# Sliding attention beside a gated MLP on one core: statistics, loads and transposes of the first tiles rearranged, and the output matmuls in another order

## The chip, the core and the metric

The kernel runs on one core of a Trainium2 chip. The core has five instruction streams that run side by side and wait for each other through semaphores: TensorE (PE: matmuls, and the loads of their weights, PEld), VectorE (DVE), ScalarE (ACT), GpSimd (POOL) and SyncE (SP, which here only issues DMAs). Matrices lie in SBUF with 128 partitions; matmuls write into PSUM, eight banks of 512 float32 columns per partition. The metric is the device time of one execution in microseconds (us), as the median of several. The profile's span is a little shorter than that time, since it starts with the first recorded work of the program.

## What is computed

`x` has 2048 tokens of 512 channels, in bfloat16, and is normalised once (`xn`). Two branches read it, and both are added to `x`.

```python
def _A_ref(x, wqkv, wo):                     # H = 32 heads of 16 channels
    W, dil = (8, 2)                          # each token sees itself and 7 tokens back, in steps of 2
    qkv = (x @ wqkv) ...
    logits = jnp.einsum('bhsd,bhswd->bhsw', q, kg) * scale
    attn = _softmax(logits, axis=-1)
    o = jnp.einsum('bhsw,bhswd->bhsd', attn, vg)
    return o ... @ wo

def _B_ref(x, w_in, w_sp, b_sp, w_out):      # F = 1376, Fh = 688
    z = _gelu(jnp.einsum('bsd,df->bsf', x, w_in))
    z1 = z[..., :Fh].copy()
    z2 = _layernorm(z[..., Fh:], axis=-1)
    g = jnp.einsum('ts,bsf->btf', w_sp, z2) + b_sp[None, :, None]
    return jnp.einsum('bsf,fd->bsd', z1 * g, w_out)
x = A_x
xn = _layernorm(x, axis=-1)
return x + _A_ref(xn, A_wqkv, A_wo) + _B_ref(xn, B_w_in, B_w_sp, B_b_sp, B_w_out)
```

## The kernel before

The tokens are 16 tiles of 128. Nothing is scheduled by a planner: each engine runs its instructions in the order in which the program text issues them (`manual_schedule`), and the tile framework adds the semaphore waits. Instructions of different engines are interleaved in the text so that a wait is short. [...]

**The front (lines 90 to 182 and 350 to 383).** SP loads tile 0, tile 1, tiles 2 and 3 together (`x0`), then `w_z2` (the right half of `w_in`, 688 KB), then tiles 4 to 7, the two halves of `wqk`, and the other tiles. ScalarE's own queue loads `b16`, which is `b_sp` as 16 rows of 128. While nothing has arrived, TensorE runs matmuls of a tile of ones (`spin`). For each of the first four tiles: `ln_stats(i)` takes mean and variance on DVE (`bn_stats`, `bn_aggr`), `roots` takes the square root on ScalarE, `recip` and `ln_apply` (DVE) make the normalised tile, `transpose_pe` turns it with four matmuls into PSUM, and a copy (ScalarE for tiles 0 and 1, DVE for 2 and 3) writes `xnT`, channels by tokens. As soon as `xnT` of a tile exists, TensorE runs its eight matmuls with `w_z2` (`z2_part`, four channel chunks times two halves of 344 columns); `z2_gelu` on ScalarE stores Gelu of the sum. PSUM for these comes from `bank_pair`, three pairs of banks in turn. `b16` is turned by a TensorE transpose (`pb`) and copied to `b_col`, one value of `b_sp` per partition for each tile.

Tiles 4 to 15 go in pairs (`groups`): statistics on DVE, an inverse root by Newton steps on DVE and POOL (`ln_newton`), and a transposing DMA on SP.

**The middle (lines 401 to 531 and 590 to 611).** Q and K (`qk_pair`, `qk_chunk`), the remaining `z2` tiles, V, the attention products, and then for each of the 16 output tiles `mix(j)` (32 matmuls with `w_sp`, which SP loads transposed as `wspT`; ScalarE adds `b_col`) and `z1_tile(j)` (eight matmuls and Gelu). `gate_out` multiplies the two on DVE and sends the product by a transposing DMA to `uT`. `vector_work` spreads the weighted sum over V on DVE between these (`av_ops`); its result is `op`, with channels grouped by position in the head. `op_rest` copies two of the 16 positions into free rows of the sixth chunk of `uT`, by eight DMAs: for the first half of the tokens on SP (line 610), for the second on ScalarE's queue (line 657).

**The output stage (lines 614 to 659).** Each output tile of 128 tokens is one PSUM bank. It gets two parts. The attention part (line 635) is 14 matmuls of 32 rows; four tiles use the four row groups of the array at once (`tile_position`), each tile in its own bank. The other part (line 646) is six full matmuls of `uT` with `wout`. Tiles are numbered by `jj` (0 to 3) and row group `k` (0 to 3). Before, a pair of `jj` is worked on at a time: attention parts of both (112 matmuls), then the full matmuls of its eight tiles, each followed by an add of `x` on DVE (line 650) and a store. So the two kinds of matmul alternate: 112 row-packed, 48 full, 112 row-packed, 42 full, and the last tile apart (`last_tile`, in two halves of 256 columns). `xr` holds the rows of `x` to add, two buffers; `ot` the results, four buffers; `rest` adds the attention part and `x` of the last tile ahead of time.

Of the kernel before, what the change touches and what calls it, by code (L numbers as in the profile page):

```python
# [7 lines left out]
BF16 = mybir.dt.bfloat16  # L8
# [37 lines left out]
def kernel(  # L46
# [42 lines left out]

    b16 = const.tile([NT, P], BF16, name="b16")  # L90
    A.dma_start(b16[:], B_b_sp.rearrange("(j p) -> j p", p=P))


# [4 lines left out]
    def spin(n):  # L98
        for _ in range(n):
            PE.matmul(idle[:, 0, 0:P], ones[:], ones[:], start=True, stop=True)  # L100

    spin(26)

# [6 lines left out]
    for c in range(C):  # L110
# [7 lines left out]
                    base=-DIL * (W - 1), pattern=[[DIL, W], [1, HALO]], channel_multiplier=0)  # L118
    b_col = const.tile([P, NT], F32, name="b_col")
    stats = const.tile([P, NT, 6], F32, name="stats")  # L120
    mv = const.tile([P, NT, 2], F32, name="mv")
# [48 lines left out]
    SP.dma_start(x0[:, 1, :], x2[P:2 * P, :])  # L170
    SP.dma_start(x0[:, 2:4, :], x2[2 * P:4 * P, :].rearrange("(i p) d -> p i d", p=P))
    SP.dma_start(w_z2[:], w_in_r[:, :, FH:F])
    xq.append(x0)
    load_x(1)
# [174 lines left out]

    pb = ps_aux.tile([P, NT], BF16, name="pb", tag="aux")  # L350
    PE.transpose(pb[:], b16[:], ident[0:NT, 0:NT])
    spin(9)
    ln_stats(0)
    roots(0, 1)
    A.copy(b_col[:], pb[:])
    ln_stats(1)
    roots(1, 2)
    recip(0)
    transpose_pe(0, ln_apply(0))
    recip(1)  # L360
    spin(4)
    transpose_pe(1, ln_apply(1))
    spin(4)
    ln_stats(2)
    roots(2, 3)
    ln_stats(3)
    roots(3, 4)
    pz0 = z2_start(0)
    z2_gelu(0, pz0)
    recip(2)  # L370
    xn2 = ln_apply(2)
    recip(3)
    xn3 = ln_apply(3)
    pz1 = bank_pair("pzb")
    for kc in range(2):
        z2_part(1, pz1, kc)
    transpose_pe(2, xn2)
    for kc in range(2, C):
        z2_part(1, pz1, kc)
    transpose_pe(3, xn3)  # L380
# [7 lines left out]
    for g in groups + (None,):  # L388
        if g:
            for i in range(*g):  # L390
                ln_stats(i)
            ln_newton(*g)
        if prev:
            for i in range(*prev):
                transpose_dma(i, ln_apply(i))
            if prev[0] == 6:
                SP.dma_start(wv[:], wqkv_r[:, :, 2 * D:3 * D])
        prev = g
# [17 lines left out]
    z2_square(5)  # L416
    qk_chunk(1, 3)
    for j in range(5):
        load_wsp(j)
        if j == 1:  # L420
            SP.dma_start(w_z1[:], w_in_r[:, :, 0:FH])
# [192 lines left out]
    def last_tile(i, rest):  # L614

        ot = otp.tile([P, D], BF16, name="ot")
        for h in range(2):
            ns = slice(h * D // 2, (h + 1) * D // 2)
            po = ps_o[0].tile([P, D], F32, name="po")
# [3 lines left out]
            V.tensor_tensor(ot[:, ns], po[:, ns], rest[:, ns], ALU.add)  # L623
            SP.dma_start(out2[i * P:(i + 1) * P, ns], ot[:, ns])


    ps_o.append(ctx.enter_context(tc.tile_pool(name="ps_o1", bufs=4, space=PSUM, side="right", reuse_waits="tile")))
    for pair in range(2):
        pos = {}
        for jj in (2 * pair, 2 * pair + 1):  # L630
            for k in range(NG):
                pos[jj, k] = ps_o[jj % 2].tile([P, D], F32, name="po")
            for d in range(DHA):
                for k in range(NG):
                    PE.matmul(pos[jj, k][:], op[32 * k:32 * k + 32, d, jj * P:(jj + 1) * P],  # L635
                              wo_r[32 * k:32 * k + 32, d, :],
                              start=(d == 0), stop=((jj, k, d) == (3, NG - 1, DHA - 1)), tile_position=(32 * k, 0))
        for jj in (2 * pair, 2 * pair + 1):
            hb, q = jj // 2, jj % 2
            for k in range(NG):  # L640
                i = 8 * hb + 2 * k + q
                if (jj, k) == (3, NG - 1):
                    last_tile(i, rest)
                    continue
                for m in range(MCH):
                    PE.matmul(pos[jj, k][:], uT[:, m, i * P:(i + 1) * P], wout[:, m, :],  # L646
                              start=False, stop=(m == MCH - 1))
                vector_work(2.0)
                ot = otp.tile([P, D], BF16, name="ot")
                V.tensor_tensor(ot[:], pos[jj, k][:], xrs[jj][:, k, :], ALU.add)  # L650
                SP.dma_start(out2[i * P:(i + 1) * P, :], ot[:])
                if (jj, k) == (2, 0):
                    rest = pwp.tile([P, D], F32, name="rest", tag="pw")
                    V.tensor_tensor(rest[:], pos[3, NG - 1][:], xrs[3][:, NG - 1, :], ALU.add)
            if jj == 0:
                vector_work(1e9)
                op_rest(1, A)
            if jj + 2 < 4:
                load_xr(jj + 2)


# [28 lines left out]
```

## Time and profile before

| | |
|---|---|
| time, median of 3 runs | 206.86 us (206.8 to 207.03) |
| time of the profiled execution | 206.6 us |
| its span | 204.9 us |
| TensorE busy | 200.3 us, 98% |
| VectorE busy | 166.1 us, 81% |
| ScalarE busy | 93.5 us, 46% |
| first matmul that the result needs (`pt`, transposes of tile 0) | 5.33 us |
| first z2 matmul (`pzb`) | 6.83 us |
| first q/k matmul (`pq`) | 11.94 us |
| output stage begins (`po`, row-packed) | 168.64 us |

The profile gives, for one execution, the instructions of each engine with start and duration from the span's start. Matmuls are pipelined: a recorded matmul of 512 columns lasts 0.38 us, but the next one starts 0.216 later, so on TensorE the distance from start to start counts. The chain of waits follows the work that ended last back to the start: what stands in it sets the end. What an engine off that chain does costs nothing until it makes the chain wait. The timeline merges equal neighbours ("x4" is four instructions), and in brackets says how long the engine was idle before and what it waited for.

### The profile page before, as it was taken

The numbers are of one execution on the slowest core, as the hardware profiler recorded it, in microseconds if no ns is written. First come the engines' busy times: TensorE is split into PE (matmuls) and PEld (weight loads), VectorE is DVE, ScalarE is ACT, GpSimd is POOL, SyncE is SP. The second block draws the span as 40 slices with busy tenths as digits, with TensorE's granted clock in tenths as the row PEclk, the third lists the DMA queues.
The fourth block names the chain that finished last, engine by engine and source line by source line (L and its number), as shares of the span: only waits on it lengthen the run. The fifth ranks groups of instructions, "written<-read, shape, count | busy, mean of one in ns | idle before, by whom it ended". The sixth has DMA issues, their size and how long they took to land.

```text
span 204.9 us, 4056 instructions
## 1 busy us (share of the span) xinstructions
PE 200.3 (98%) x1660; PEld 120.7 (59%) x1666; DVE 166.1 (81%) x192; ACT 93.5 (46%) x145; POOL 16.1 (8%) x82
## 2 busy tenths in 40 slices
PE   7999999999999999999999999999999999999994
PEld 7755554555566666656666666666666664444442
DVE  4899949659299599989999999999999985582353
ACT  3868897676879996335733331213333320000000
POOL 5045630000000000100000000000000000000000
PEclk9999999999999999999999999999999999999999
DMA  6973846999000004718766799999565225047323
GB/s 170 363 223 78 198 95 154 213 212 117 4 3 0 3 0 44 154 32 163 122 129 141 179 210 187 218 175 187 114 145 140 56 48 80 26 99 218 110 99 97
DMA packets 67395, 25.64 MB, mean 125 GB/s; under 512 B 57152, under 2 KB 67248, under 8 KB 67248
## 3 DMA queue, kind: packets, MB, share of 16 engines
q1 hardware_dynamic: 66960, 25.24, 57.6%
q8 instruction: 13, 0.21, 0.4%
q10 hardware_dynamic: 416, 0.14, 0.3%
q14 instruction: 6, 0.05, 0.1%
HBM read 9.79 MB, written 2.10 MB: 58 GB/s over the span
## 4 chain that ended last, share of the span: by engine, by line
PE 96%; DVE 1%; DMA 1%; issue 0%
PE pg L492 36%; PE pq L260 10%; PE po L646 9%; PE pzb L229 9%; PE pz L504 9%; PE pv L285 7%; PE po L635 6%; PE pl L310 4%; PE pq L272 3%; DMA xq<-in_A_x_dram 1%; PE po L621 1%; PE pt L212 1%; DVE stats L185 1%; PE idle L100 0%; DVE xn L190 0%
## 5 line engine op out<-in xcount | busy, mean ns | idle before, releaser
L492 PE MATMUL pg<-z,wspT 128*128 128x344 bf16 x512 | 77.3, 309 | 0.0
L492 PEld LDWEIGHTS <-wspT 128*128 128x128 bf16 x512 | 50.0, 98 | 24.9 <-issue 0.4
L301 DVE TENSOR_TENSOR pr<-qk 128x8192 bf16<-128x8192 bf16 x8 | 35.0, 4420 | 7.4 <-PE pl L310 7.4
L495 ACT ACTIVATE gs<-pg,b_col 128x688 bf16<-128x688 f32 x16 | 13.3, 833 | 52.9 <-PE pg L492 52.9
L558 DVE TENSOR_TENSOR pw<-vp,a_sb 128x4096 bf16<-128x4096 bf16 x16 | 36.1, 2284 | 0.0
L650 DVE TENSOR_TENSOR ot<-po,xr 128x512 bf16<-128x512 f32 x15 | 10.2, 689 | 15.2 <-PE po L646 14.9
L260 PE MATMUL pq<-xnT,wqk 128*128 128x512 bf16 x93 | 21.4, 379 | 0.2
L504 PE MATMUL pz<-w_z,xnT 128*128 128x344 bf16 x128 | 21.3, 309 | 0.0
L229 PE MATMUL pzb<-w_z,xnT 128*128 128x344 bf16 x128 | 20.1, 309 | 0.0
L646 PE MATMUL po<-wout,uT 128*128 128x512 bf16 x88 | 19.3, 379 | 0.3 <-issue 0.3
L563 DVE TENSOR_TENSOR pw<-pw 128x4096 bf16<-128x4096 bf16 x8 | 18.3, 2288 | 0.1
L229 PEld LDWEIGHTS <-xnT 128*128 128x128 bf16 x128 | 12.3, 98 | 7.0 <-issue 0.4
L504 PEld LDWEIGHTS <-xnT 128*128 128x128 bf16 x128 | 12.4, 98 | 6.5 <-issue 0.4
L260 PEld LDWEIGHTS <-wqk 128*128 128x128 bf16 x96 | 9.3, 98 | 10.9 <-issue 0.4
L646 PEld LDWEIGHTS <-uT 128*128 128x128 bf16 x90 | 8.6, 98 | 11.0 <-issue 0.8
L263 ACT CAST qk<-pq 128x1024 bf16<-128x1024 f32 x12 | 12.1, 1012 | 5.4 <-PE pq L260 5.4
L285 PE MATMUL pv<-xnT,wv 128*32 128x512 bf16 x256 | 14.6, 380 | 0.0
L509 ACT ACTIVATE z<-pz 128x688 bf16<-128x688 f32 x16 | 11.9, 743 | 5.6 <-PE pz L504 5.2
L238 ACT ACTIVATE junk<-z 128x688 bf16<-128x688 bf16 x16 | 12.4, 778 | 0.2
L635 PE MATMUL po<-wo_r,op 32*128 32x512 bf16 x224 | 12.4, 375 | 0.0
L234 ACT ACTIVATE z<-pzb 128x688 bf16<-128x688 f32 x16 | 11.8, 735 | 1.4 <-PE pzb L229 1.4
L285 PEld LDWEIGHTS <-wv 128*32 128x32 bf16 x256 | 9.4, 139 | 4.6 <-issue 0.3
(81 smaller groups left out, 169.2 us busy)
## 6 DMA issues: line engine op xcount, KB each, us to landing
xr<-in_A_x_dram SPq DMA_DIRECT2D x4, 512.0 KB, 4.1
out_dram<-ot SPq DMA_DIRECT2D x15, 128.0 KB, 1.8
wo_r<-in_A_wo_dram SPq DMA_DIRECT2D x4, 448.0 KB, 4.8
w_z<-in_B_w_in_dram SPq DMA_DIRECT2D x2, 688.0 KB, 4.9
xq<-in_A_x_dram SPq DMA_DIRECT2D x2, 512.0 KB, 7.0
wqk<-in_A_wqkv_dram SPq DMA_DIRECT2D x2, 512.0 KB, 7.0
wout<-in_B_w_out_dram SPq DMA_DIRECT2D x1, 640.0 KB, 5.2
a_sb<-in_A_x_dram SPq DMA_DIRECT2D x1, 512.0 KB, 9.1
```

Source lines behind the costliest of these rows:

```text
L229: PE.matmul(pz[:, hh, 0:FHALF], xnT[:, kc, i * P:(i + 1) * P], w_z2[:, kc, hh * FHALF:(hh + 1) * FHALF], start=(kc == 0), stop=(kc == C - 1))
L238: A.activation(junk[:], z2[:, i, :], ACT.Square, accum_out=zsq[:, i:i + 1])
L260: PE.matmul(pq[:, s, :], wqk[:, kc, s, c * P:(c + 1) * P], xnT[:, kc, tsl], start=(kc == 0), stop=(kc == C - 1))
L285: PE.matmul(pv[32 * k:32 * k + 32, dd, :].rearrange("p (b t) -> p b t", b=NB), wv_v[:, kc, 2 * d2 + dd, :], xnT_g[:, kc, :, k, :], start=( ...
L301: V.tensor_tensor(pr[:], qk[hb][:, 0, :, HALO:HALO + SB].unsqueeze(1).broadcast_to([P, 2, C, SB]), shifted(qk[hb][:, 1, :, off:off + SB]), ...
L492: PE.matmul(pg[:, hh, 0:FHALF], wsps[j][:, k, :], z2[:, k, hh * FHALF:(hh + 1) * FHALF], start=(k == 0), stop=(k == NT - 1))
L495: A.activation(gs[:], pg[:, :, 0:FHALF], ACT.Identity, bias=b_col[:, j:j + 1])
L504: PE.matmul(pz[:, hh, 0:FHALF], xnT[:, kc, j * P:(j + 1) * P], w_z1[:, kc, hh * FHALF:(hh + 1) * FHALF], start=(kc == 0), stop=(kc == C - 1))
L558: V.tensor_tensor(pw[:], shifted(vp[:, :, hb, off:off + P]), a_sb[:, 2 * p:2 * p + 2, osl].unsqueeze(2).broadcast_to([P, 2, DH, P]), ALU.mult)
L563: V.tensor_tensor(pws[p - 1][:], pws[p - 1][:], pw[:], ALU.add)
L635: PE.matmul(pos[jj, k][:], op[32 * k:32 * k + 32, d, jj * P:(jj + 1) * P], wo_r[32 * k:32 * k + 32, d, :], start=(d == 0), stop=((jj, k, d ...
L646: PE.matmul(pos[jj, k][:], uT[:, m, i * P:(i + 1) * P], wout[:, m, :], start=False, stop=(m == MCH - 1))
```

## The change

The diff has three parts.

Front: tile 3 is loaded by itself, after `w_z2`. The mean and variance of tile 1 are taken on ScalarE with two activations that add up along the row (Identity with scale −1/512 gives the negative mean; Square with that as bias gives the summed squared deviations), and its normalisation adds the negative mean. A square root of a constant is ScalarE's first instruction. The order of the first tiles' instructions is new: on TensorE, the first four z2 matmuls of tile 0 stand before the transposes of tile 1, and two more before those of tile 2. `ln_stats(4)` is moved ahead. The idle matmuls are 35 and 5, where there were 26, 9, 4 and 4.

`b_sp`: no DMA on ScalarE's queue and no transpose on TensorE; a transposing DMA on SP, placed after the twelve transposing DMAs of `xnT` and before the loads of `wspT`, and a copy on POOL.

Output stage: the full matmuls of the eight tiles of `jj` 0 and 1 come first, then the attention parts of all four `jj` in one row of 224 matmuls, then the full matmuls of the other tiles. The adds and stores of `jj` 0 and 1 follow their attention part. All of DVE's remaining attention work and the second `op_rest` stand before the first add. The last tile is as it was.

```diff
@@ -87,9 +87,6 @@
         pool = ps_b if turn[0] % 3 == 0 and not two else ps_a
         return pool.tile([P, 2, 512], F32, name=name, tag="mm")
 
-    b16 = const.tile([NT, P], BF16, name="b16")
-    A.dma_start(b16[:], B_b_sp.rearrange("(j p) -> j p", p=P))
-
 
     ones = const.tile([P, P], BF16, name="ones")
     V.memset(ones[:], 1.0)
@@ -99,7 +96,7 @@
         for _ in range(n):
             PE.matmul(idle[:, 0, 0:P], ones[:], ones[:], start=True, stop=True)
 
-    spin(26)
+    spin(35)
 
     ident = const.tile([P, P], BF16, name="ident")
     G.memset(ident[:], 0.0)
@@ -117,6 +114,7 @@
     G.affine_select(out=mask[:], in_=mask[:], compare_op=ALU.is_ge, fill=NEG,
                     base=-DIL * (W - 1), pattern=[[DIL, W], [1, HALO]], channel_multiplier=0)
     b_col = const.tile([P, NT], F32, name="b_col")
+    b_t = const.tile([P, NT], BF16, name="b_t")
     stats = const.tile([P, NT, 6], F32, name="stats")
     mv = const.tile([P, NT, 2], F32, name="mv")
     rstd = const.tile([P, NT], F32, name="rstd")
@@ -168,8 +166,9 @@
     x0 = xqp.tile([P, 4, D], BF16, name="xq")
     SP.dma_start(x0[:, 0, :], x2[0:P, :])
     SP.dma_start(x0[:, 1, :], x2[P:2 * P, :])
-    SP.dma_start(x0[:, 2:4, :], x2[2 * P:4 * P, :].rearrange("(i p) d -> p i d", p=P))
+    SP.dma_start(x0[:, 2, :], x2[2 * P:3 * P, :])
     SP.dma_start(w_z2[:], w_in_r[:, :, FH:F])
+    SP.dma_start(x0[:, 3, :], x2[3 * P:4 * P, :])
     xq.append(x0)
     load_x(1)
     for s in range(2):
@@ -347,36 +346,37 @@
     def recip(i):
         V.reciprocal(rstd[:, i:i + 1], rstd[:, i:i + 1])
 
-    pb = ps_aux.tile([P, NT], BF16, name="pb", tag="aux")
-    PE.transpose(pb[:], b16[:], ident[0:NT, 0:NT])
-    spin(9)
+    A.activation(zrstd[:, 0:1], eps_t[:], ACT.Sqrt)
     ln_stats(0)
+
+    A.activation(junk[:, 0:D], x0[:, 1, :], ACT.Identity, scale=-1.0 / D, accum_out=mv[:, 1, 0:1])
     roots(0, 1)
-    A.copy(b_col[:], pb[:])
-    ln_stats(1)
-    roots(1, 2)
+    A.activation(junk[:, 0:D], x0[:, 1, :], ACT.Square, bias=mv[:, 1, 0:1], accum_out=mv[:, 1, 1:2])
+    A.activation(rstd[:, 1:2], mv[:, 1, 1:2], ACT.Sqrt, bias=eps_t[:], scale=1.0 / D)
     recip(0)
     transpose_pe(0, ln_apply(0))
+    spin(5)
+    ln_stats(2)
     recip(1)
-    spin(4)
-    transpose_pe(1, ln_apply(1))
-    spin(4)
-    ln_stats(2)
+    xn1 = xnp.tile([P, D], BF16, name="xn")
+    V.tensor_scalar(xn1[:], x0[:, 1, :], mv[:, 1, 0:1], rstd[:, 1:2], ALU.add, ALU.mult)
     roots(2, 3)
+    pz0 = bank_pair("pzb")
+    for kc in range(2):
+        z2_part(0, pz0, kc)
+    transpose_pe(1, xn1)
+    recip(2)
+    xn2 = ln_apply(2)
     ln_stats(3)
     roots(3, 4)
-    pz0 = z2_start(0)
+    z2_part(0, pz0, 2)
+    transpose_pe(2, xn2)
+    z2_part(0, pz0, 3)
     z2_gelu(0, pz0)
-    recip(2)
-    xn2 = ln_apply(2)
     recip(3)
     xn3 = ln_apply(3)
-    pz1 = bank_pair("pzb")
-    for kc in range(2):
-        z2_part(1, pz1, kc)
-    transpose_pe(2, xn2)
-    for kc in range(2, C):
-        z2_part(1, pz1, kc)
+    ln_stats(4)
+    pz1 = z2_start(1)
     transpose_pe(3, xn3)
     z2_gelu(1, pz1)
     z2_tile(2)
@@ -388,7 +388,8 @@
     for g in groups + (None,):
         if g:
             for i in range(*g):
-                ln_stats(i)
+                if i > 4:
+                    ln_stats(i)
             ln_newton(*g)
         if prev:
             for i in range(*prev):
@@ -415,6 +416,8 @@
     qk_chunk(1, 2)
     z2_square(5)
     qk_chunk(1, 3)
+    SP.dma_start_transpose(b_t[:], B_b_sp.rearrange("(j p) -> j p", p=P))
+    G.tensor_copy(b_col[:], b_t[:])
     for j in range(5):
         load_wsp(j)
         if j == 1:
@@ -614,51 +617,67 @@
     def last_tile(i, rest):
 
         ot = otp.tile([P, D], BF16, name="ot")
-        for h in range(2):
-            ns = slice(h * D // 2, (h + 1) * D // 2)
+        for q, n0, n1 in ((SP, 0, 256), (SP, 256, 512)):
+            ns = slice(n0, n1)
             po = ps_o[0].tile([P, D], F32, name="po")
             for m in range(MCH):
                 PE.matmul(po[:, ns], uT[:, m, i * P:(i + 1) * P], wout[:, m, ns],
                           start=(m == 0), stop=(m == MCH - 1))
             V.tensor_tensor(ot[:, ns], po[:, ns], rest[:, ns], ALU.add)
-            SP.dma_start(out2[i * P:(i + 1) * P, ns], ot[:, ns])
+            q.dma_start(out2[i * P:(i + 1) * P, ns], ot[:, ns])
+
 
 
     ps_o.append(ctx.enter_context(tc.tile_pool(name="ps_o1", bufs=4, space=PSUM, side="right", reuse_waits="tile")))
-    for pair in range(2):
-        pos = {}
-        for jj in (2 * pair, 2 * pair + 1):
+    pos = {}
+
+    def tokens_of(jj, k):
+        return 8 * (jj // 2) + 2 * k + jj % 2
+
+    def out_b(jj, k, first):
+        i = tokens_of(jj, k)
+        if first:
+            pos[jj, k] = ps_o[jj % 2].tile([P, D], F32, name="po")
+        for m in range(MCH):
+            PE.matmul(pos[jj, k][:], uT[:, m, i * P:(i + 1) * P], wout[:, m, :],
+                      start=first and m == 0, stop=not first and m == MCH - 1)
+
+    def out_a(jj, first):
+        for k in range(NG):
+            if first:
+                pos[jj, k] = ps_o[jj % 2].tile([P, D], F32, name="po")
+        for d in range(DHA):
             for k in range(NG):
-                pos[jj, k] = ps_o[jj % 2].tile([P, D], F32, name="po")
-            for d in range(DHA):
-                for k in range(NG):
-                    PE.matmul(pos[jj, k][:], op[32 * k:32 * k + 32, d, jj * P:(jj + 1) * P],
-                              wo_r[32 * k:32 * k + 32, d, :],
-                              start=(d == 0), stop=((jj, k, d) == (3, NG - 1, DHA - 1)), tile_position=(32 * k, 0))
-        for jj in (2 * pair, 2 * pair + 1):
-            hb, q = jj // 2, jj % 2
+                PE.matmul(pos[jj, k][:], op[32 * k:32 * k + 32, d, jj * P:(jj + 1) * P],
+                          wo_r[32 * k:32 * k + 32, d, :], start=first and d == 0,
+                          stop=(not first or (jj, k) == (3, NG - 1)) and d == DHA - 1, tile_position=(32 * k, 0))
+
+    def store(jj, k):
+        i = tokens_of(jj, k)
+        ot = otp.tile([P, D], BF16, name="ot")
+        V.tensor_tensor(ot[:], pos[jj, k][:], xrs[jj][:, k, :], ALU.add)
+        SP.dma_start(out2[i * P:(i + 1) * P, :], ot[:])
+
+    for jj in range(2):
+        for k in range(NG):
+            out_b(jj, k, True)
+    vector_work(1e9)
+    op_rest(1, A)
+    for jj in range(4):
+        out_a(jj, jj > 1)
+        if jj < 2:
             for k in range(NG):
-                i = 8 * hb + 2 * k + q
-                if (jj, k) == (3, NG - 1):
-                    last_tile(i, rest)
-                    continue
-                for m in range(MCH):
-                    PE.matmul(pos[jj, k][:], uT[:, m, i * P:(i + 1) * P], wout[:, m, :],
-                              start=False, stop=(m == MCH - 1))
-                vector_work(2.0)
-                ot = otp.tile([P, D], BF16, name="ot")
-                V.tensor_tensor(ot[:], pos[jj, k][:], xrs[jj][:, k, :], ALU.add)
-                SP.dma_start(out2[i * P:(i + 1) * P, :], ot[:])
-                if (jj, k) == (2, 0):
-                    rest = pwp.tile([P, D], F32, name="rest", tag="pw")
-                    V.tensor_tensor(rest[:], pos[3, NG - 1][:], xrs[3][:, NG - 1, :], ALU.add)
-            if jj == 0:
-                vector_work(1e9)
-                op_rest(1, A)
-            if jj + 2 < 4:
-                load_xr(jj + 2)
-
-
+                store(jj, k)
+            load_xr(jj + 2)
+    rest = pwp.tile([P, D], F32, name="rest", tag="pw")
+    V.tensor_tensor(rest[:], pos[3, NG - 1][:], xrs[3][:, NG - 1, :], ALU.add)
+    for jj in range(2, 4):
+        for k in range(NG):
+            if (jj, k) == (3, NG - 1):
+                last_tile(tokens_of(jj, k), rest)
+            else:
+                out_b(jj, k, False)
+                store(jj, k)
```

## The prediction

> **What bounds the kernel now.** I read the page's shares and chain first, then the chain in order of time, then the timeline of the two places that the change touches. Page and chain:
>
> ```profile
> PE 200.3 (98%) x1660; PEld 120.7 (59%) x1666; DVE 166.1 (81%) x192; ACT 93.5 (46%) x145; POOL 16.1 (8%) x82
> PE 96%; DVE 1%; DMA 1%; issue 0%
> ```
>
> ```profile
> 4.86 0.42 DVE xn L190
> ...
> 5.33 0.61 PE pt L212 x4
> 5.94 0.43 PE idle L100 x4
> 6.37 0.26 PE pt L212 x4
> 6.63 0.22 PE idle L100 x4
> 6.85 1.90 PE pzb L229 x12
> ...
> 168.71 6.16 PE po L635 x112
> 174.87 0.16 issue
> 175.03 10.31 PE po L646 x47
> 185.33 6.15 PE po L635 x112
> 191.49 0.16 issue
> 191.65 9.01 PE po L646 x41
> ```
>
> From 6.85 to 201.98 the chain never leaves TensorE. Time can be won only by (a) starting the useful stream before 6.85, (b) taking matmuls or gaps out of it. It can be lost by any new wait in it. Now the front by timeline:
>
> ```profile
> 1.26 0.42 SPq L170 DMA_DIRECT2D xq<-in_A_x_dram  x1
> ...
> 2.19 0.47 SPq L172 DMA_DIRECT2D w_z<-in_B_w_in_dram  x1
> ...
> 4.02 0.29 ACT L194 ACTIVATE rstd<-mv,eps_t 128x1 f32<-128x1 f32 x1 [1.49 <-DVE mv L186]
> ...
> 4.69 0.13 DVE L348 RECIPROCAL rstd<-rstd 128x1 f32<-128x1 f32 x1
> ...
> 6.63 1.76 PEld L229 LDWEIGHTS <-xnT 128*128 128x128 bf16 x12
> 6.83 1.91 PE L229 MATMUL pzb<-w_z,xnT 128*128 128x344 bf16 x12
> ```
>
> Two things meet at 6.8. The weights from xnT are loaded at 6.63, when ScalarE's copy is done, but the matmul starts at 6.83. The DMA list gives w_z2 4.6 us from issue to landing: 2.19 + 4.6 = 6.79. So w_z2 ends last, 0.2 behind xnT of tile 0. Also, rstd of tile 0 is there at 4.31, but its reciprocal waits until 4.69 behind tile 1's statistics on DVE.
>
> **The change, part by part.**
>
> *Tile 1's statistics to ScalarE.* DVE loses bn_stats and bn_aggr of tile 1 (0.66 + 0.18). ScalarE gains a spare root at the start (0.29, behind the table load, before any data), an Identity and a Square with accumulators, and no longer copies b_col (0.17). Tile 1 lands at 1.26 + 2.2 = 3.46. No row shows Identity over 512 elements with an accumulator. Nearest: Square over 688 (0.78, its accumulator read starting 0.68 in and taking 0.19) and the copy of 512 (0.585). I take 0.63 and 0.10 for the part of the read that follows. Tile 0's root then starts at 4.19 instead of 4.02 and ends at 4.48. Its reciprocal no longer queues behind anything on DVE: 4.50 instead of 4.69. All that follows moves by 0.19: normalised tile 4.67, transposes 5.14, copy on ScalarE 5.79, xnT of tile 0 at 6.42 (was 6.61). Bounds: with the 688 rows unscaled (0.87 together) the root is 0.14 later and the gain 0.05; with 0.585 and no read after it, 0.33. Square and the second root end near 5.5, ahead of that copy.
>
> [...]
>
> *w_z2 ahead of tile 3.* Tiles 2 and 3 landed at 1.72 + 3.2 = 4.92, the 688 KB of w_z2 1.87 later, so 128 KB less ahead is worth 0.35 us: landing at about 6.45. It could be less, as the transfer is issued no earlier (2.19) and the queue ran at only 98 GB/s from 3.1 to 3.6, waiting for issues: between 0.15 and 0.35, I take 0.31. Tile 3 lands at about 6.8 instead of 4.92. Only its bn_stats waits for it, in DVE's order behind tile 2's normalisation, which ends near 7.3: hidden by 0.5. SP issues one DMA more (0.42), so tiles 4 to 7, wqk and the two later groups are issued 0.42 later. The first wqk half landed about 3.25 + 7.0 = 10.25; with 0.42 it is 10.7, and TensorE wants it at 11.9.
>
> *First z2 matmul.* Both inputs now arrive at 6.42 to 6.48: it starts at about 6.50, 0.33 earlier.
>
> *From there to the q/k matmuls (11.94 now).* The stretch before held 32 matmuls at 0.146 and eight transposes at 0.055: 4.67 + 0.44 = 5.11, exactly 6.83 to 11.94, no waits. The new order holds twelve transposes there, since tile 1's moved from the covered time into the stream: 5.33, so 11.83. Waits: transposes of tile 1 at 7.08 (its input is ready near 6.44) end at 7.47; ScalarE's copy (0.63) gives xnT at 8.13. z2 of tile 1 would start at 8.11, so it starts at about 8.20: 0.09 lost. Tile 2's normalised input (7.3) is wanted at 7.6, tile 3's (9.1) at 9.4. The Gelu table load moves from 7.76 to about 8.5, the first Gelu ends near 10.55, and its bank is wanted at 10.75. Sum: 11.92 against 11.94. The front gives **0.02**: the 0.33 is spent on 0.22 of transposes that had been free and 0.09 of a new wait. Bounds: 0.25 gained (landing and statistics at their better ends, copy in 0.42 as DVE does it) to 0.2 lost.
>
> *b_sp.* The ACT-queue DMA, TensorE's transpose and the copy go; SP issues one more transposing DMA before the first wspT, POOL one small copy. On SP such a DMA takes 5.36 / 4 = 1.34. Behind it stand five wspT loads (from 31.85) and w_z1, the first wanted at 73.3: nothing, and 1.3 without that cover. POOL's next instruction, a memset for the gate, is 40 us away.
>
> *The output stage.* Matmul counts stay: 224 row-packed, 88 full. Start to start, 168.64 to 185.27 holds 28 rounds of four and eight tiles: 16.63. From 185.27 to the last tile at 200.50 it holds 28 rounds and seven tiles: 15.23. One tile is 1.296 (residual adds at 194.22, 195.52, 196.81), so the first has 0.10 more: the step back into packed mode. 15.23 − 7 × 1.296 = 6.16 for 28 rounds; at the full matmul's pitch of 0.216 they are 6.05, so stepping out costs 0.11. One pair of steps goes: **0.21**. Bounds: 0, if packed rounds are really slower and the step in was a bank waiting for DVE; 0.52, if all of the 0.42 idle of the weight loader before L646 is a step.
>
> New waits there: full matmuls of tiles 0 to 7 now start at 168.6 and need op rows that SP issues from 159.76 to 164.78 and lands 1.8 later: 2 us of cover at the start. DVE's last products (2.28 + 2.28 + 1.22 from 170.01) end at 175.8; the packed stretch starts at 179.0. Its third part takes over the first part's banks 6.05 after the stretch began; four residual adds start 3.2 in and take 2.5, end 5.7: 0.3 of cover. The second four need ot buffers whose stores were issued 2.3 earlier and land in 1.8: 0.5 of cover. The x rows of the last four tiles are issued near 188.2 and land at 192.3; the early sum for the last tile waits for them on DVE about a microsecond, and DVE has caught up two tiles later at 1.3 per tile against 0.69. The tail is unchanged.
>
> **Sum.** 0.02 + 0.21 = 0.23 off. The profiled execution took 206.6 (span 204.9, 1.7 around it), 0.26 under the median of 206.86; I carry the saving over: **206.6**. Its own range is 206.1 to 207.05 (0.77 gained to 0.2 lost). A difference under 0.2% (0.41 us) is about what a measurement of this kernel can't tell from no change.
>
> **Rivals.**
> *The front passes through.* The earlier start reaches the q/k matmuls (0.25) and two mode steps are worth 0.3: 0.55, 206.3. For it: w_z2 was the last arrival, and all terms are at bounds that rows allow. Against: four transposes are no longer covered. 0.25.
>
> *No part does what it says.* If rounds are slower in themselves and the front's gain is spent: 206.85. 0.1.
>
> *TensorE warms up later: slower.* Weight loads of the idle matmuls take 0.15 until 6.2 and 0.10 after:
>
> ```profile
> 6.05 0.15 PEld L212 LDWEIGHTS <-xn 128*128 128x128 bf16 x1
> ...
> 6.41 0.10 PEld L100 LDWEIGHTS <-ones 128*128 128x128 bf16 x1
> ```
>
> The array runs at half pace for some 5.1 us from its first matmul (1.12). Before, matmuls filled the time up to 6.83. Now five idle ones end near 6.1 and nothing follows until 6.5, just where the pace changed. If the change comes x later, x / 2 is lost; over 0.41 from x = 1.3. Starting anew it would be 5.1 later: 209.1. Against it: gaps of 0.3 near 5.0 were there before as well. 0.08.
>
> [...]
>
> *Stores too slow: slower.* If the stores land in 3.1 (as the op rows on ACT's queue do) instead of 1.8, the second four adds are 0.8 late and the fourth packed part waits: 207.4. 0.06.
>
> The forecast itself has 0.51, mostly within 0.2%. Faster: 0.25 plus a small part of the forecast's lower edge, 0.28; slower: 0.14; within: 0.58. The range 206.1 to 207.1 leaves out the two slower cases and little else.
>
> **What would show it.** First z2 matmul near 6.5; first q/k matmul at 11.8 to 12.0 (under 11.7 the front passes through, over 12.3 the clock or a wait); ScalarE's first Identity near 3.5 and tile 0's root near 4.2; one packed stretch of 12.2 with no gap at its third and fourth part; its start at 179.0. I am wrong if TensorE idles inside that stretch, or if the first loads after 6.5 still take 0.15.

## The result, and the profile after

The changed kernel takes 207.63 us (median of 21 executions, 206.99 to 209.42) against 206.78 (21 executions, 206.47 to 207.96) on the same chip: a ratio of 1.0044, 95% interval 1.0028 to 1.0059. It is 0.85 us slower, outside the range of the prediction. Its profiled execution took 207.34, span 205.6 (before: 206.6 and 204.9).

The page's shares and the tail of the chain of waits in order of time (start, length, what):

```profile
PE 200.7 (98%) x1662; PEld 120.9 (59%) x1662; DVE 165.5 (80%) x190; ACT 94.8 (46%) x149; POOL 17.7 (9%) x83
...
PE 93%; DMA 4%; DVE 1%; SPq 1%; issue 0%; DVEq 0%
```

```profile
179.25 5.67 PE po L651 x101
184.93 2.77 DMA out_dram<-ot
187.72 0.05 DVEq L658
187.77 1.29 DVE ot L658 x2
189.11 3.18 PE po L651 x53
```

TensorE is still busy 98% of the span, so the shares show nothing. The chain does: it leaves TensorE in the middle of the packed stretch. A store of the output lands, two residual adds follow, and only then do the last 53 packed matmuls start. The timeline of the same place:

```profile
179.18 9.70 PE L651 MATMUL po<-wo_r,op 32*128 32x512 bf16 x171
...
182.41 2.48 DVE L658 TENSOR_TENSOR ot<-po,xr 128x512 bf16<-128x512 f32 x4 [6.35 <-PE po L651]
183.13 3.11 SPq L659 DMA_DIRECT2D out_dram<-ot  x4
185.43 0.69 DVE L658 TENSOR_TENSOR ot<-po,xr 128x512 bf16<-128x512 f32 x1 [0.54 <-PE po L651]
...
187.17 1.89 DVE L658 TENSOR_TENSOR ot<-po,xr 128x512 bf16<-128x512 f32 x3 [1.04 <-DMA out_dram<-ot]
...
189.11 3.18 PE L651 MATMUL po<-wo_r,op 32*128 32x512 bf16 x53 [0.23 <-DVE ot L658]
```

The first four adds run in one piece. Of the second four one runs, and the next waits 1.04 for its `ot` buffer: there are four, and it is the sixth add, so it needs the second store to have landed. The chain names the fourth store (launched at 184.93), because the wait for it ended just before the add at 187.77. But from 187.17 on the adds start 0.60 apart, as the first four do, so it is the second store's landing that sets them. The fourth packed part takes the banks that these adds free. From the start of the stretch (179.18) to the next full matmul (192.22) it is 13.04; without the hole it is 12.20 in an experiment below, so the hole is 0.84.

The front in the same view:

```profile
2.18 0.43 SPq L170 DMA_DIRECT2D w_z<-in_B_w_in_dram  x1
...
3.45 0.63 ACT L352 ACTIVATE junk<-xq 128x512 bf16<-128x512 bf16 x1 [1.16 <-DMA xq<-in_A_x_dram]
...
4.08 0.28 ACT L193 ACTIVATE rstd<-mv,eps_t 128x1 f32<-128x1 f32 x1
...
5.06 0.61 PE L211 MATMUL pt<-ident,xn 128*128 128x128 bf16 x4
...
6.34 0.10 PEld L228 LDWEIGHTS <-xnT 128*128 128x128 bf16 x1 [0.43 <-ACT xnT L213]
6.75 0.74 PE L228 MATMUL pzb<-w_z,xnT 128*128 128x344 bf16 x4 [0.66 <-DMA w_z<-in_B_w_in_dram]
7.33 0.39 PE L211 MATMUL pt<-ident,xn 128*128 128x128 bf16 x4
...
8.38 0.99 PEld L228 LDWEIGHTS <-xnT 128*128 128x128 bf16 x8 [0.22 <-ACT xnT L213]
...
12.12 3.19 PE L271 MATMUL pq<-xnT,wqk 128*128 128x512 bf16 x14
```

Tile 0's weights are loaded at 6.34, earlier than before (6.63), but w_z2 lands only at 2.18 + 4.52 = 6.70, against 6.79. The first z2 matmul gains 0.08 and the q/k matmuls start at 12.12, 0.18 later than before (11.94).

So, at the last tile's matmul (200.50 before, 201.29 now, +0.79): +0.18 from the front, still +0.19 where the output stage begins, then +0.84 for the hole and about 0.22 less for the mode steps.

### The profile page after: what moved, and what is told of

It is laid out like the page before. It is cut to its first block, busy times and chain, and to the rows that moved or that the text cites. A ratio compares the mean times of both kernels' runs of the same rounds, so it can differ in the third digit from the quotient of the medians.

```text
span 205.6 us, 4063 instructions
## 1 busy us (share of the span) xinstructions
PE 200.7 (98%) x1662; PEld 120.9 (59%) x1662; DVE 165.5 (80%) x190; ACT 94.8 (46%) x149; POOL 17.7 (9%) x83
## 4 chain that ended last, share of the span: by engine, by line
PE 93%; DMA 4%; DVE 1%; SPq 1%; issue 0%; DVEq 0%
PE pg L495 36%; PE pq L259 10%; PE po L642 9%; PE pzb L228 9%; PE pz L507 9%; PE pv L284 7%; PE po L651 4%; PE pl L309 4%; PE pq L271 3%; DMA w_z<-in_B_w_in_dram 2%; DMA out_dram<-ot 1%; PE po L624 1%; DVE ot L658 1%; PE pt L211 0%; SPq L169 0%; DVE ot L626 0%
## 5 line engine op out<-in xcount | busy, mean ns | idle before, releaser
L642 PE MATMUL po<-wout,uT 128*128 128x512 bf16 x90 | 19.8, 379 | 0.0
L228 PEld LDWEIGHTS <-xnT 128*128 128x128 bf16 x128 | 12.2, 98 | 7.6 <-issue 0.7
L651 PE MATMUL po<-wo_r,op 32*128 32x512 bf16 x224 | 12.9, 374 | 0.2 <-DVE ot L658 0.2
```

The costliest lines, as they stand in the source:

```text
L228: PE.matmul(pz[:, hh, 0:FHALF], xnT[:, kc, i * P:(i + 1) * P], w_z2[:, kc, hh * FHALF:(hh + 1) * FHALF], start=(kc == 0), stop=(kc == C - 1))
```

## Experiments

Each kernel was timed beside the kernel before, whose medians were 206.68 to 206.74. Where no range is given, the time is that of a single execution.

### The output stage: four result buffers

**stage_only**: the kernel before with the change's new output stage (its last hunks, from `last_tile` on) and the old front.

```
-    for pair in range(2):
...
+    for jj in range(4):
+        out_a(jj, jj > 1)
+        if jj < 2:
+            for k in range(NG):
+                store(jj, k)
```

> The kernel before with the new output stage alone (front and b_sp as before). Theory (result buffers): the stage costs 0.6, so 207.35 to 207.5 against 206.78, with the same DVE wait for out_dram<-ot. Rival (the front is to blame): no slower than before, 206.5 to 206.8.

207.29 (207.21 to 208.08, 6 executions), ratio 1.0038 (1.0023 to 1.0052). The sixth add waits 0.93 for a store, and TensorE's last packed matmuls start late as in the changed kernel. The loss of 0.6 is in the output stage.

**after_ot7**: the changed kernel with seven result buffers.

```
-    otp = ctx.enter_context(tc.tile_pool(name="otp", bufs=4, reuse_waits="tile", **right))
+    otp = ctx.enter_context(tc.tile_pool(name="otp", bufs=7, reuse_waits="tile", **right))
```

> The changed kernel with seven ot buffers instead of four; nothing else. Theory (result buffers): the second four adds of the output stage wait for stores of the first four (1.04 us of DVE idle named to out_dram<-ot), and the fourth packed part waits for these adds. With seven buffers the wait goes, the packed stretch is one piece of about 12.2 us, and the time falls by 0.6 to 0.85 to 206.8 to 207.0. Rival (banks or the row-packed matmuls themselves): the hole in the stretch stays and the time stays near 207.6. Second rival (the whole loss is the front or a later clock): under 0.2 of gain.

206.70 (206.46 to 208.3, 11), ratio 0.9998 (0.9977 to 1.0019): 0.93 under the changed kernel. The second store still lands after 3.4, but no add waits for it. The timeline has one packed piece, and both groups of adds run through:

```profile
179.36 12.27 PE L651 MATMUL po<-wo_r,op 32*128 32x512 bf16 x224
...
185.61 2.48 DVE L658 TENSOR_TENSOR ot<-po,xr 128x512 bf16<-128x512 f32 x4 [0.54 <-PE po L651]
...
191.56 9.24 PE L642 MATMUL po<-wout,uT 128*128 128x512 bf16 x42
```

**after_ot5**: the same with `bufs=5`, a single execution.

> The changed kernel with five ot buffers. Theory (result buffers; stores issued 0.6 apart land after 1.8, 3.3, 3.0, 2.8): the second add of the second four needs the first store, which is early; the third needs the second store, landed near 187.05, and would be due at 186.6: a wait of 0.4 against 1.04, of which the fourth packed part sees 0.1 to 0.25 after its cover of 0.3. Rival (any stall comes from the PSUM banks): the same wait as with four.

207.23. The wait moves from the sixth to the seventh add and shrinks to 0.59, and the stretch lasts 12.65 instead of 12.27. The hole halves to 0.38, more than the 0.1 to 0.25 expected.

```profile
185.75 1.29 DVE L658 TENSOR_TENSOR ot<-po,xr 128x512 bf16<-128x512 f32 x2 [0.54 <-PE po L651]
187.63 1.29 DVE L658 TENSOR_TENSOR ot<-po,xr 128x512 bf16<-128x512 f32 x2 [0.59 <-DMA out_dram<-ot]
```

**stage_ot7**: stage_only with `bufs=7`, so that nothing but the mode steps differs from before.

> The kernel before with the new output stage and seven ot buffers. This is the price of the two mode steps by itself. Theory: 0.2 off the kernel before, 206.5 to 206.65. Rival (steps between packed and full matmuls cost nothing): 206.75 to 206.85. Rival (they cost the 0.42 that the weight loader idles): 206.3.

206.55 (206.14 to 207.07, 11), ratio 0.9994 (0.9985 to 1.0003). From the last input matmuls (167.83; before 167.82) to the last tile (200.29; before 200.50) it is 0.22 shorter: the predicted price of one pair of steps. In the times it is 0.15, not clear of no change.

### Why the stores land late

The DMA view gives each store of the first four by itself (launched at 183.1, 183.7, 184.3 and 184.9; last column: us to landing), and the kinds of packets in a window (packets, MB, share of 16 engines). Of the changed kernel, the first two stores, the window 184 to 185 and the window 185.6 to 186.2:

```profile
out_dram<-ot SPq DMA_DIRECT2D x1, 128.0 KB, 1.8
...
out_dram<-ot SPq DMA_DIRECT2D x1, 128.0 KB, 3.3
...
q8 instruction: 1, 0.02, 8.0%
...
DMA packets 11, 0.01 MB, mean 9 GB/s; under 512 B 6, under 2 KB 11, under 8 KB 11
```

The first store lands after 1.8, the second after 3.3, the next two after 3.0 and 2.8. Between them lies one packet of kind "instruction" on queue 8. 8.0% of 16 engines for 1 us is 1.28 us on one engine, from 184.59 on. After it the queue all but stands for 0.6 us: single packets, 0.1 apart, as of one engine that is behind the other fifteen. The packets of 4 bytes, of which each store has sixteen, fit this estimate: fifteen of the second store's start between 184.95 and 185.09, the last at 186.55. Such 16 KB packets appear 13 times in a span with 3,344 TensorE instructions: one per 257. That they are TensorE's code is an estimate from this count, and no row names it; the next experiments add and take away TensorE instructions and see whether the packet moves.

The profile of before had it too, in rows that the prediction didn't read: one packet at 180.29, the second store landing after 3.0, and the sixth add already waiting. Its DMA view (180 to 181, then the store launched at 179.8) and its timeline:

```profile
q8 instruction: 1, 0.02, 8.7%
...
out_dram<-ot SPq DMA_DIRECT2D x1, 128.0 KB, 3.0
```

```profile
182.95 0.69 DVE L650 TENSOR_TENSOR ot<-po,xr 128x512 bf16<-128x512 f32 x1 [0.22 <-DMA out_dram<-ot]
```

The three kernels below leave stores and buffers as in the changed kernel and only change how many idle matmuls, and of what length, fill the first 4 us of TensorE (after_few and after_mid also fill the tile that these read).

**after_few** (52 TensorE instructions fewer) and **after_mid** (34 fewer, a single execution):

```
-    spin(35)
...
+    V.memset(z2[:, NT - 1, 0:512], 1.0)
+    for _ in range(9):
+        PE.matmul(idle[:, 0, 0:512], ones[:], z2[:, NT - 1, 0:512], start=True, stop=True)
```

(after_mid: 256 for 512 and 18 for 9.) **after_more** (70 instructions more, a single execution):

```
-    spin(35)
+    for _ in range(70):
+        PE.matmul(idle[:, 0, 0:64], ones[:], ones[:, 0:64], start=True, stop=True)
```

> The changed kernel, four output buffers, with its 35 first idle matmuls of 128 columns replaced by 9 of 512: the same time on TensorE, 26 matmuls and 26 weight loads fewer. The profile shows a 16 KB packet of kind instruction on queue q8 about once per 256 TensorE instructions (13 packets for 3344), one of them at 184.9, lasting 1.28 us on one DMA engine, just while the second store's bytes move. Code-load theory: that packet, not the closeness of the stores, makes stores 2 to 4 land in 3.3, 3.0 and 2.8. With 52 instructions fewer it comes 52 / 36.7 per us = 1.4 us later, at about 186.3 (0.8 either way): the first three stores land in 1.7 to 2.2, the second four adds wait under 0.3 for a store (was 1.04), the packed stretch has a hole of 0.2 at most (was 0.84), 206.8 us. Rival, stores 0.6 apart are slow in themselves: landings of 1.8, 3.3, 3.0, a wait of 1.0, a hole of 0.8, 207.6 us, wherever the packet comes.

> The same with 18 idle matmuls of 256 columns: 34 TensorE instructions fewer, so the packet comes some 0.9 us later, at 185.8. Code-load theory: at the mean the second and third store land in about 2 and only the fourth or the next is late; wait 0 to 0.6 for a store, hole 0 to 0.4. Rival: wait 1.0, hole 0.8.

> The changed kernel with 70 idle matmuls of 64 columns in place of 35 of 128: 70 TensorE instructions more, so the packet comes 1.9 us earlier, at about 183.0 in the changed kernel's times (the front may start later where the 70 don't fit into 3.9 us; that moves all times alike). Code-load theory: the packet is over at 184.2, just after the first store's bytes start to move: first store in 1.8 to 2.3, the others under 2.3, wait under 0.3, hole under 0.2. Rival: wait 1.0, hole 0.8.

- after_more: 206.49. The packet comes at 182.56, all four stores land in 1.8 to 1.9 though they are as close as before, nothing waits for them, and there is no hole.
- after_mid: 206.66. The packet comes at 186.59, 0.8 later than expected. The four stores land in 1.7, 1.7, 1.7 and 2.0; no wait, no hole.
- after_few: 208.25 (206.96 to 208.5, 6), a miss in its time, its wait and its hole. The packet comes at 187.03, at the late end of what was expected. Stores one to three land in 1.7 to 1.8 as expected, but the fourth lands after 4.0, and the eighth add waits 1.69 for it.

The timelines of after_few and after_more:

```profile
185.75 1.89 DVE L660 TENSOR_TENSOR ot<-po,xr 128x512 bf16<-128x512 f32 x3 [0.54 <-PE po L653]
...
189.33 0.69 DVE L660 TENSOR_TENSOR ot<-po,xr 128x512 bf16<-128x512 f32 x1 [1.69 <-DMA out_dram<-ot]
190.07 3.18 PE L653 MATMUL po<-wo_r,op 32*128 32x512 bf16 x53 [1.11 <-DVE ot L660]
```

```profile
179.12 12.27 PE L652 MATMUL po<-wo_r,op 32*128 32x512 bf16 x224
...
185.37 2.48 DVE L659 TENSOR_TENSOR ot<-po,xr 128x512 bf16<-128x512 f32 x4 [0.54 <-PE po L652]
```

So it isn't the closeness of the stores. Which store is late moves with the packet: the second with the packet at 184.59, the fourth at 187.03, none at 182.56 or 186.59. How near a packet must come isn't settled. after_mid's starts 1.53 after the fourth store's launch and costs it 0.2 to 0.3. after_few's starts 1.79 after, when fifteen of the store's sixteen packets of 4 bytes have come (by 186.65), and the last is late all the same. What held it until 187.03, and why the store took 4.0 in all, the trace doesn't say.

**after_more_t**: after_more again, with times.

> after_more again, with times: does it hold over executions that the hole goes when the code packet lies ahead of the stores, with four buffers as in the changed kernel? Code-load theory: median 206.5 to 206.9, at least 0.7 under the changed kernel's 207.63. Rival: 207.6.

206.53 (206.41 to 207.0, 12), ratio 0.9993 (0.9984 to 1.0002): 1.1 under the changed kernel, with four buffers and no useful instruction changed. That is 0.26 more than the hole in the changed kernel's profile, though the q/k matmuls start as late as there (12.10). The execution profiled there (207.34) lies under its median (207.63), so the usual hole may be larger; no trace shows it. The packet was again between 182.5 and 183, and the stores landed in 1.7 to 1.8.

### The front

**front_only**: the changed kernel's front and b_sp with the old output stage.

```
+    SP.dma_start(x0[:, 2, :], x2[2 * P:3 * P, :])
     SP.dma_start(w_z2[:], w_in_r[:, :, FH:F])
+    SP.dma_start(x0[:, 3, :], x2[3 * P:4 * P, :])
...
+    A.activation(junk[:, 0:D], x0[:, 1, :], ACT.Identity, scale=-1.0 / D, accum_out=mv[:, 1, 0:1])
```

> The kernel before with the new front and the new way of b_sp, output stage as before. Theory (profile of the change): the front is 0.18 late at the first q/k matmul, so about 206.95, with single executions 1.7 higher when TensorE's full pace comes one interval later, as three of the 21 of the changed kernel were. Rival (front neutral): 206.78 and no such executions.

206.93 (206.55 to 209.21, 11), ratio 1.0021 (0.9995 to 1.0048): 0.23 slower, not clear by itself. Two of the eleven took 208.57 and 209.21 at a mean granted clock of 0.992, 1.64 and 2.28 above the median. No run shows the interval of the expectation; what the runs show is three executions of the changed kernel 1.68 to 1.79 above its median of 207.63, and 3.4 us at half pace in front_wz3 (below). In its profile w_z2 landed 4.8 after issue and the q/k matmuls started at 12.44.

**front_t1**: front_only with tile 1's transposes ahead of the first z2 matmuls, where TensorE waits for w_z2 anyway.

```
+    transpose_pe(1, xn1)
     for kc in range(2):
         z2_part(0, pz0, kc)
-    transpose_pe(1, xn1)
```

> The new front alone, with the transposes of tile 1 ahead of the first four z2 matmuls of tile 0. Theory (TensorE idles until w_z2 lands, and the four transposes behind that point are paid in full): 0.2 less than the new front alone, 206.7, level with the kernel before. Rival (the transposes are hidden where they are): no change, 206.9.

206.55 (206.3 to 206.68, 10), ratio 0.9997 (0.9988 to 1.0006): 0.38 under front_only, though the two intervals overlap.

```profile
6.30 0.40 PE L211 MATMUL pt<-ident,xn 128*128 128x128 bf16 x4 [0.64 <-DVE xn L362]
6.87 1.03 PE L228 MATMUL pzb<-w_z,xnT 128*128 128x344 bf16 x6 [0.17 <-DMA w_z<-in_B_w_in_dram]
...
11.98 2.32 PE L271 MATMUL pq<-xnT,wqk 128*128 128x512 bf16 x9
```

The transposes run at 6.30 under the wait for w_z2, and q/k starts at 11.98 although z2 starts at 6.87: 5.11 from one to the other, as in the kernel before, against 5.37 in the changed kernel. The traces agree on this: it is 5.37 or 5.38 in all nine with the changed order at full clock and one transfer for w_z2, and 5.10 or 5.11 in the four with front_t1's edit.

**front_split**: front_only with w_z2 in two transfers.

```
-    SP.dma_start(w_z2[:], w_in_r[:, :, FH:F])
+    SP.dma_start(w_z2[:, 0:2, :], w_in_r[:, 0:2, FH:F])
+    SP.dma_start(w_z2[:, 2:4, :], w_in_r[:, 2:4, FH:F])
```

> The new front alone, with w_z2 loaded by two DMAs of two channel chunks each, one after the other at the same place. Theory (the front waits for w_z2, and a transfer starts a fixed time after its own issue): the first half is issued at 2.18 and lands near 5.8 instead of 6.7 to 7.0, so the first z2 matmul starts when tile 0's xnT is there, at 6.0 to 6.4, and the second half (near 6.9) is in time for the third chunk. The first q/k matmul moves from 12.1 to 12.4 to 11.6 to 11.8, the time 0.4 to 0.6 under the new front alone, to 206.4. Rival (xnT or something else sets the start): no gain, 206.9.

A miss: 207.06 (206.68 to 207.47, 12), ratio 1.0016 (1.0005 to 1.0028). The halves landed after 3.3 and 3.7 and z2 started at 6.30, but tile 3 was queued behind both and landed 4.1 after issue:

```profile
6.30 0.76 PE L229 MATMUL pzb<-w_z,xnT 128*128 128x344 bf16 x4
...
7.28 0.69 DVE L185 BATCH_NORM_STATS2 stats<-xq 128x6 f32<-128x512 bf16 x1 [0.20 <-DMA xq<-in_A_x_dram]
...
11.98 2.32 PE L272 MATMUL pq<-xnT,wqk 128*128 128x512 bf16 x9
```

Of 0.77 gained on front_only at z2, 0.46 was left at q/k in this execution, which at 206.68 was the fastest of the twelve, and the median shows none of it. Why isn't settled.

**front_wz3**: front_only with w_z2 ahead of tile 2 as well, a single execution. **front_nospin**: front_only without the five idle matmuls. **front_fill**: fifteen of them.

```
-    SP.dma_start(x0[:, 2, :], x2[2 * P:3 * P, :])
     SP.dma_start(w_z2[:], w_in_r[:, :, FH:F])
+    SP.dma_start(x0[:, 2, :], x2[2 * P:3 * P, :])
```

```
-    spin(5)
```

```
-    spin(5)
+    spin(15)
```

> The new front alone, with w_z2 issued ahead of tile 2 as well. It is a look at one landing. Theory (fixed time from its own issue to the start of its bytes): issued at 1.71 instead of 2.18, it lands 0.45 earlier, at 6.1 to 6.5, again 4.4 to 4.8 after its issue. Rival (the landing follows the bytes ahead of it at some 370 GB/s, 0.35 for 128 KB): with 128 KB less ahead than in the new front, 0.35 earlier than that, and 4.8 after the issue or more. Tile 1's normalisation stands behind tile 2's statistics on VectorE and gets later, so the time is no better.

> The new front alone, without the five idle matmuls between tile 0's transposes and the first z2 matmuls, so that TensorE idles about 1.3 us there instead of 0.7. It tells whether the idle time ahead of w_z2 brings back half pace, as the one look at the earlier w_z2 issue showed (granted clock 0.50 from 8 to 11 us after 1.84 us of idling). Theory (clock): many executions, a third or more, are 1 to 2 us above the new front alone (206.9), the fastest stay near 206.7. Rival (the slow single executions are something else): the same share as with the five, one in seven or fewer.

> The new front alone, with 15 idle matmuls there instead of five, so that TensorE is busy until 6.2 to 7.1. Theory (clock): no executions 1 us or more above the rest, spread as in the kernel before, median 206.8 to 206.95. Rival: one in seven stays at 208.5 to 209.4.

- front_wz3: 209.52, a miss. w_z2, issued at 1.71, landed 5.7 later, and TensorE stood idle for 1.84.
- front_nospin: 209.07 (208.03 to 211.15, 6), ratio 1.0115 (1.0062 to 1.0168). In its profile TensorE stood idle for 3.04. Even the fastest was 1.3 above the 206.7 expected of it, and three of the six, of 208.03 to 210.67, have a mean granted clock of 1.0: the clock isn't all of this loss.
- front_fill: 206.91 (206.62 to 207.75, 12), ratio 1.0007 (0.9988 to 1.0027): little different from front_only, and none 1 us above the rest, as expected. w_z2 landed 5.3 after issue in its profile.

What followed the idle time stands in the windows view (stretch, its length, busy time of PE, PEld, DVE, ACT and POOL, then the granted clock, the DMA share and GB/s). front_wz3, then front_nospin:

```profile
7.00:8.00 1.00, 0.52 (x3) 0.34 (x3) 0.23 (x1) 0.00 (x0) 0.00 (x0) 0.87 1.03 362
8.00:9.00 1.00, 0.57 (x3) 0.00 (x0) 0.93 (x4) 0.29 (x1) 0.00 (x0) 0.50 1.04 369
...
11.00:12.00 1.00, 1.00 (x8) 0.64 (x7) 0.96 (x4) 1.00 (x1) 0.00 (x0) 0.93 1.09 386
```

```profile
7.00:8.00 1.00, 0.00 (x0) 0.00 (x0) 0.00 (x0) 0.00 (x0) 0.00 (x0) 0.60 1.08 358
...
13.00:14.00 1.00, 1.00 (x6) 0.48 (x4) 0.09 (x1) 0.26 (x2) 0.00 (x0) 0.50 0.33 114
```

A mean of 0.87 over 1 us is 0.26 at half pace, so the clock is halved from about 7.74 to 11.14 in the first and from 7.20 to beyond 14 in the second. 3.4 us at half pace is at most 1.7 lost. From the first z2 matmul to q/k it is 7.43 in front_wz3 and 7.99 in front_nospin, against 5.37 in front_only; in front_wz3 a wait of 0.66 for tile 1's normalised rows is part of that.

### Both causes removed

**best_t1**: the changed kernel with `bufs=7` and front_t1's edit. **best_fill**: best_t1 with eight idle matmuls before tile 1's transposes and five after. **more_t1**: after_more with front_t1's edit, four buffers.

```
-    spin(5)
+    spin(8)
...
     transpose_pe(1, xn1)
+    spin(5)
```

> The changed kernel with seven ot buffers and with tile 1's transposes ahead of the first z2 matmuls. Theory: both losses are mended; the front is level with or 0.1 ahead of the kernel before, the output stage 0.2 ahead: 206.3 to 206.45 against 206.7. Rival (the parts do not add): 206.55 to 206.7.

> The same with eight idle matmuls before tile 1's transposes instead of five, and five after them. Theory: median as the one before or up to 0.1 later, no execution 1 us above the rest. Rival (idle matmuls only push the useful ones back): 0.1 to 0.3 later.

> after_more with tile 1's transposes ahead of the first z2 matmuls, four output buffers. If the front's loss is those transposes (front_t1: 0.36) and the hole stays away: 206.2 to 206.5, below the kernel before. If the code packet comes back into the stores in many executions: 206.6 to 207.3, with a wide spread.

206.55 (206.06 to 208.55, 12), ratio 0.9994 (0.997 to 1.0019); 206.46 (206.32 to 207.21, 12), ratio 0.9983 (0.9964 to 1.0002); 206.36 (206.14 to 207.38, 12), ratio 0.9988 (0.9977 to 1.0). All three medians lie below the kernel before, more_t1 by 0.35 with an interval that just reaches no change. best_t1 lies at the edge of what its rival expected, that the parts don't add (206.55 to 206.7).

## Why the prediction was wrong

| step | predicted | measured |
| --- | --- | --- |
| tile 0's root starts | 4.19 | 4.08 |
| xnT of tile 0 | 6.42 | 6.34 |
| w_z2 lands | 6.48 | 6.70 |
| first z2 matmul | 6.50 | 6.75 |
| from there to q/k | 5.33 + 0.09 | 5.37 |
| first q/k matmul | 11.92 | 12.12 |
| packed stretch | 12.2, no gap | 13.04, gap of 0.84 |
| one pair of mode steps | 0.21 | 0.22 (stage_ot7) |

*The failed step* is the cover in the output stage: "The second four need ot buffers whose stores were issued 2.3 earlier and land in 1.8: 0.5 of cover." The second to fourth store landed in 3.3, 3.0 and 2.8, with a 16 KB packet of kind "instruction" that took 1.28 on one DMA engine. Where the packet lay at 182.56 or 186.59, these stores landed in 1.8 to 1.9 (after_more) and 1.7 to 2.0 (after_mid), and its place moves with the number of TensorE instructions ahead of it (182.56 with 70 more, 187.03 with 52 fewer). The cover of 0.5 was worked out from the usual landing, where the trace of before held a landing of 3.0 and an add that waited for it.

*The rival "Stores too slow"* said that the second four adds would be 0.8 late and the fourth packed part would wait: 207.4. The place and the size were right (0.84). The row it argued from, the op rows on ACT's queue, wasn't the cause, and it got too small a chance.

*The front.* The order's cost was foreseen; "I take 0.31" for w_z2 was mis-sized. It landed 0.09 earlier than before, below the stated bound of 0.15, and even that may be luck: over the kept traces it landed at 6.56 to 6.79 with the old loads (three) and at 6.64 to 7.02 with the new ones (twelve; front_fill and front_nospin later still). The sum divided 128 KB by the rate of a full queue (w_z2's 688 KB in 1.87). The DMA rate in windows of 0.2 us, before and then after (columns as above):

```profile
3.60:3.80 0.20, 0.20 (x5) 0.20 (x2) 0.17 (x1) 0.00 (x0) 0.19 (x1) 1.00 0.95 323
3.80:4.00 0.20, 0.20 (x3) 0.00 (x1) 0.20 (x2) 0.00 (x0) 0.14 (x1) 1.00 1.08 381
```

```profile
3.60:3.80 0.20, 0.20 (x5) 0.20 (x3) 0.17 (x2) 0.20 (x1) 0.20 (x1) 1.00 1.08 62
3.80:4.00 0.20, 0.20 (x5) 0.20 (x4) 0.07 (x1) 0.20 (x2) 0.12 (x1) 1.00 0.13 48
```

Without tile 3 ahead, w_z2's packets (the only ones of 1,376 bytes) start at 3.33 instead of 3.97, but from 3.6 to 4.0 the queue moves only 62 and 48 GB/s. w_z2's packets pass 300 GB/s from 4.4 on, as in the kernel before, and the last of them starts at 6.24, there at 6.27. The prediction read its slow stretch (98 GB/s from 3.1 to 3.6) as waiting for issues; here w_z2 had been issued by 2.62. Why the transfer starts so slowly is open. So the 0.22 of transposes and a wait at tile 1's copy (0.04, where 0.09 was foreseen) were bought with 0.08 instead of 0.33. front_t1 shows that the order made the loss: with the transposes under the wait it is gone.

*Statistics on ScalarE.* Right: the Identity took the 0.63 assumed, the root came 0.11 earlier than said. The Square over the same 512 elements took 0.71.

*b_sp.* Nothing, as said: the lag of 0.18 at the q/k matmuls is 0.19 at the output stage.

*Mode steps.* Right in size: 0.22 in the trace of stage_ot7. In the times alone it isn't clear of no change.

*The clock rival.* Not the cause: the median loss is accounted for without it. But front_wz3 and front_nospin show it as real and close. The paces that it starts from are in the trace of before: 26 idle matmuls of 128 columns took 2.96 from 1.12 on (0.106 apart), four took 0.39 from 6.46 on (0.057 apart). In front_wz3 the half-pace time of 3.4 is worth up to 1.7; in front_nospin, where it lasted twice as long, q/k was 2.6 later after the first z2 matmul. In front_wz3 half pace followed a gap of 1.84; after the changed kernel's gap of 0.66 at this place the granted clock stayed at 1.00. That the gap is its cause is inferred from these runs alone. Of the changed kernel's 21 executions three took 209.3 to 209.4; one has a mean granted clock of 0.992, and for the other two the cause is open.

*The front passes through; no part does what it says.* Both fell: q/k started later, and the mode steps did pay, by the trace of stage_ot7.

With the measured terms in the prediction's sum (206.86 − 0.23 = 206.63): 206.63 + 0.84 for the hole + 0.20 for the front (0.18 lost in place of 0.02 gained) = 207.67, against 207.63. That it fits to 0.04 is partly luck, since the terms come from one execution, of 207.34.

## What to carry to other kernels

Where a ring of buffers is freed by stores, take the cover against the slowest landing that the trace holds, not the median, and look for a row that already waits for it. Here the "instruction" packet moved with the number of TensorE instructions ahead of it (182.56 to 187.03), and with it at 184.59 or 187.03 some of the first four stores landed in 2.8 to 4.0 instead of 1.7 to 2.0: give such a ring slack instead of tuning against the packet's place. Taking 128 KB out from ahead of w_z2 moved the start of its first packet by 0.64 and that of its last by 0.03; look at both. And a wait that stays is the place for work that must be done anyway, such as tile 1's transposes here.

## What the runs showed of the hardware

- A 16 KB packet of kind "instruction" on queue 8 takes 0.9 to 1.4 us on one DMA engine (the changed kernel's 13) and comes about once per 257 TensorE instructions (13 in 3,344). In the changed kernel the three 128 KB stores behind it took 2.8 to 3.3 us to landing, in other versions single ones took up to 4.0; without it there they took 1.7 to 2.0. Its place moves by 0.6 us between versions with the same TensorE instructions (184.59 in the changed kernel, 185.20 in after_ot7), which may be part of the scatter of the times; that wasn't tried.
- Stores 0.6 apart on one queue aren't slow in themselves: four landed in 1.8 to 1.9 each (after_more).
- w_z2 took 4.4 to 6.3 us to land in kernels that issue it almost alike (4.8 in front_only, 5.3 in front_fill, 6.3 in front_nospin). No "instruction" packet lies there (the changed kernel's first 16 KB one starts at 13.00). In front_nospin it is as if one engine were late: all but 25 of the 512 packets have started by 6.09, and the rest start one by one, 0.055 apart, from 6.76 to 8.09. Why remains open.
